# PSUM tiles for the first two chunks of a fused attention and channel-mix kernel: one tile of four banks, or one tile for each use with the four-bank tile laid over them later

## The chip, the cores and the metric

One core of a Trainium2 chip runs the kernel. The metric is device time in microseconds (us) for one execution; the median of the runs is given. Engines are called PE or TensorE (matrix products; PEld is its weight load), DVE or VectorE, ACT or ScalarE, POOL or GpSimd, and SP, which issues the DMAs. SBUF is the on-chip memory, and PSUM, of eight banks, is the memory that TensorE writes its products to. L12 is line 12 of the kernel.

## What is computed

Eight batches of 576 tokens go through attention with 8 heads of 64 against 72 keys and values, each the mean of 8 neighbours, and the result goes through a channel mix of width 512 with 1024 hidden units:

```
attn = softmax(q @ mean8(k).T / 8) @ mean8(v)          # q, k, v: [8, 8, 576, 64]
x    = attn, heads side by side                         # [8, 576, 512]
xk   = mu_k * x + (1 - mu_k) * x_prev                   # x_prev: x of the token before
xr   = mu_r * x + (1 - mu_r) * x_prev
out  = sigmoid(xr @ w_r) * (relu(xk @ w_k) ** 2 @ w_v)  # w_k: 512 x 1024, w_v: 1024 x 512, w_r: 512 x 512
```

## The kernel before

The 4608 tokens are worked in chunks of 128, 256 and then eleven of 384, and each chunk in tiles of 128 tokens: tile 0 is chunk 0, tiles 1 and 2 are chunk 1, tiles 3 to 5 chunk 2. For a tile, `softmax` and `part` make the scores on TensorE (`scores`, L791 and L799), then maxima (L839), subtraction (L856), exponential, sums and normalised weights. For a chunk, the attention product follows, and each product is turned by `shifted` (two ScalarE copies, scaled, L1080) and `joined` (two VectorE operations that read the same product again, L1122) into the two inputs xk and xr of the channel mix; `hidden` (L1177), `gate` (L1226) and `mixed` (L1259) are its matrix products.

The first two chunks take another way through PSUM than the rest. Their weights are transposed on TensorE (`transposed`, L933, and `transposed_rest`, L979) and copied to SBUF by ScalarE (L940, L986), and `attended` makes the attention product one pair of heads at a time (four pairs, L1066). Each of these uses one PSUM bank for a short while; they are called the small products here. From chunk 2 on VectorE transposes, and `quarters` (L1028) makes the product of all four pairs at once over four banks.

No instruction waits by hand. The order in which each engine gets its instructions is written out by a planner (`Order`, L131 to L241) while the kernel is built. Every piece of work is a generator. It says what it needs (`need`), takes a buffer from a list of free ones (`take`, with a kind such as "bank" or "sc") and names the engine and the length of the next step. Each generator has a due time, corrected by the table `EARLIER`. In each round the planner goes through the generators in the order of their due times and lets each take what is free; then, of the steps that are ready, it issues the one with the lowest due time on the engine that can start first. Of several free buffers of a kind it gives the one that has been free longest. The semaphores are added afterwards, from the tiles that the instructions read and write.

Four of the eight banks are one tile, `quad` (L378). Its banks 0 and 1 are handed out as the kind "sc", for the scores of a tile. Its banks 2 and 3 are handed out as two slots of the kind "bank", for the small products, and a tile of its own, `single`, is the third. `filling` takes `single` for the 40 filler products of L449, which run between the others until 47.43 us; so until then the small products alternate between banks 2 and 3. Three more banks, "mm", serve the channel mix. When the first two chunks are through, `four_banks` (L714) takes the three "bank" slots and gives banks 2 and 3 on as the kind "hi". `quarters` takes "sc" and "hi" together, and so do the scores of several tiles at once (through the view `wide`, L712). `single` becomes a fourth "mm" slot later.

What is due around this place: `gathered` of tile 3, which gives "sc" back, at 34 plus 232.6; `four_banks` at 18 plus 265.3; the scores of tile 4 at 39.4 plus 504.7.

Of the kernel before, what the change touches and what calls it, by code (L numbers as in the profile page):

```python
# [8 lines left out]
F32 = mybir.dt.float32  # L9
# [5 lines left out]
PSUM = bass.MemoryType.PSUM  # L15

P = 128
B, H, S, D = 8, 8, 576, 64
POOL = 8
KEYS = S // POOL  # L20
# [45 lines left out]
APART = 296  # L66
# [194 lines left out]
def attention_then_channel_mix(  # L261
# [15 lines left out]
    order = Order()  # L277
    need = lambda *what: ("need", *what)
    take = lambda kind: ("take", kind)
# [3 lines left out]
    banks = ctx.enter_context(tc.tile_pool(name="banks", bufs=1, space=PSUM))  # L283

    def slots(kind, n, shape, dtype=F32, pool=None):
        tiles = [(pool or const).tile(shape, dtype, name=f"{kind}{i}") for i in range(n)]
        for t in tiles:
            order.give(kind, t)
        return tiles
# [27 lines left out]
    def operand(kind, c):  # L317
        if c in WHOLE:
            return whole_operands[kind]
        if (kind, c) not in operands:  # L320
            whole = {"pth": range(len(CHUNKS)), "xkh": WHOLE_HID, "xrh": WHOLE_GATE, "sh": WHOLE_MIX, "ptq": range(len(CHUNKS))}.get(kind, ())
            dtype = F32 if c in whole else F32R
            operands[kind, c] = sb.tile(shapes[kind], dtype, name=f"{kind}_{c}", tag=kind)
        return operands[kind, c]
# [40 lines left out]
    for tag, n in EARLY:  # L365
        t = sb.tile([P, n, 2 * POOL * KEYS], F32, name=f"early_{tag}", tag=tag)
        for i in range(n):
            got = t[:, i]
# [6 lines left out]
        else:  # L375
            order.give(kind, slot)

    quad = banks.tile([P, 4, 512], F32, name="quad")  # L378
    order.give("sc", quad[:, :2])
    single, = slots("bank", 1, [P, 512], pool=banks)  # L380
    for a in (2, 3):
        order.give("bank", quad[:, a])
    slots("mm", 3, [P, 512], pool=banks)


    def stretches(at, n):
# [322 lines left out]
        done_with(kind, raw)  # L709
        order.make(("late rest", b))  # L710

    wide = quad.rearrange("p (a b) n -> p a (b n)", a=2)  # L712

    def four_banks():  # L714
        yield need(
            *[(k, i) for i, t in enumerate(tiles) if t[0] in WHOLE_ATT for k in ("main", "side")],
            *[("x", c, g, m) for c in WHOLE_ATT for g in range(NPAIR) for m in range(2)], "filled",
        )
        got = []
        for _ in range(3):  # L720
            got.append((yield take("bank")))
        order.give("hi", quad[:, 2:])
        yield need(("gating", FOURTH_FROM, 0))
        order.give("mm", single)

    def group_of(i):
        if i >= THREES_FROM:
            return [j for j, t in enumerate(tiles) if t[0] == tiles[i][0]]
        return list(TOGETHER) if i in TOGETHER else [i]

    def follows(i):
        return group_of(i)[0] != i

    def softmax(i):

        parts = tiles[i][2]
        if follows(i):
            yield need(("scores", i, 0))
            yield from part(i, 0, 2)
            return  # L740
        group = group_of(i)
        several = len(group) > 1
        if i:
            yield need(("scoring", i - 1))
            c = tiles[i if i >= THREES_FROM else max(group[-1] - 2, 0)][0] - 1
            if c >= 0 and c not in WHOLE_ATT:
                yield need(("attended", c, 0))
        yield need(*[("q", j) for j in group])
        yield need(
            *[("keys", b, p) for j in group for b, *_ in tiles[j][2] for p in range(1 if i in HALVED else 2)]  # L750
        )
        if several:
            held["four", tiles[i][0]] = [(yield take("sc")), (yield take("hi")), len(group)]
            for n, j in enumerate(group):
                view = wide[:, :, n * APART:n * APART + 4 * KEYS]
                held["halves", j] = view, None, [view[:, a:a + 1] for a in range(2)]
                order.make(("scoring", j))
            yield from part(i, 0, 2)
            return
        pair = None  # L760
        if i in BESIDE:
            pair = [(yield take("mm")), (yield take("mm"))]
            sc = None
            halves = [t.rearrange("p (a n) -> p a n", a=1) for t in pair]
        else:
            sc = yield take("sc")
            halves = [sc[:, a:a + 1] for a in range(2)]
        held["halves", i] = sc, pair, halves
        if i in HALVED:
            for kind in ("mx", "e", "sm", "px", "pm"):  # L770
                held[kind, i] = yield take(kind)
        order.make(("scoring", i))
        if i in HALVED:
            yield from part(i, 0, 1)
        else:
            yield from part(i, 0, 2)
# [224 lines left out]
    def ready(c):  # L1001
        mine = [i for i, t in enumerate(tiles) if t[0] == c]
        return (
            *[(k, i) for i in mine for k in ("main", "side")], "om",
            *([("rest", 0)] if c in WHOLE_ATT else [("late rest", b) for b, *_ in units[c]]),
            *[("values", b, p) for b, *_ in units[c] for p in range(2)], *([] if c in WHOLE_ATT else [("turned", b) for b, *_ in units[c]]),
        )

    def quarters(c):

        yield need(*ready(c))
        sc = yield take("sc")
        hi = yield take("hi")
        yield "pe", 2.75, False
        main = operand("pth", c).rearrange("p g n -> p (g n)").rearrange("p (i j k) -> p i j k", j=16, k=32)
        rest = operand("ptq", c)
        out = quad[:, :, :CH].rearrange("p t (g i k) -> p t g i k", g=NPAIR, k=32)
        batch = [next(b for b, _, n, at in units[c] if at <= CH // 4 * t < at + n) % 2 for t in range(4)]
        for g in range(NPAIR):
            for j in range(3):  # L1020
                for t, i in enumerate(batch):
                    rows = slice(32 * t, 32 * t + 32)
                    for m in range(2):
                        if j < 2:
                            w, p = vq_main[i][rows, (t - 2 * m - j) % 4, g], main[rows, :, 4 * g + 2 * m + j, :]
                        else:
                            w, p = vq_rest[i][rows, g // 2, 2 * (g % 2) + m], rest[rows, :, g // 2, :]
                        nc.tensor.matmul(  # L1028
                            out=out[m * D:(m + 1) * D, t, g], lhsT=w, rhs=p, start=(j == 0), stop=(j == 2),
                        )  # L1030
        for g in range(NPAIR):
            held["out", c, g] = quad[:, :, g * CH // 4:(g + 1) * CH // 4]
            order.make(("attended", c, g))
        held["quad", c] = [sc, hi, NPAIR]
# [265 lines left out]
    for i in range(NT):  # L1300
        spare = SPARE_THREE if i >= THREES_FROM else SPARE if tiles[i][0] > 1 else 0.0
        order.add(tile_due[i], softmax(i), spare)
        order.add(tile_due[i], gathered(i))
        if i in HALVED:
            order.add(tile_due[i] + 0.05, part(i, 1, 2), spare)
        order.add(tile_due[i] + 0.1, transposed(i), spare)
        order.add(tile_due[i] + 0.1, transposed_rest(i), spare)
    order.add(ATT[1] + 8, four_banks())
    for c, n in enumerate(CHUNKS):
        if c not in WHOLE_ATT:  # L1310
            order.add(att_due[c], quarters(c), SPARE)
        for g in range(NPAIR):
            order.add(att_due[c] + g, attended(c, g), SPARE if c > 1 else 0.0)
            if c in WHOLE:
                order.add(att_due[c] + g + 6, later_joined(c, g))
        for jt in range(NJT):
            order.add(begin[c] + 0.0455 * n * jt / NJT, hidden(c, jt), 1.0 if c else 0.0)
        for tt in range(n // P):
            order.add(begin[c] + 0.0455 * n + 2.8 * tt, gate(c, tt))
            order.add(begin[c] + (0.0455 + 0.022) * n + 5.5 * tt, mixed(c, tt))  # L1320
# [56 lines left out]
```

## Time and profile before

| | |
|---|---|
| median of 3 runs | 604.08 us (602.74 to 604.32) |
| profiled execution | 603.56 us, of which the span from the first to the last instruction is 601.7 us |
| TensorE busy | 590.3 us (98% of the span), 5822 products |
| VectorE, ScalarE, GpSimd busy | 347.7 (58%), 294.4 (49%), 223.4 (37%) |
| granted TensorE clock, mean | 0.999 |
| DMA | 54.72 MB, mean 91 GB/s |

Busy time is the time in which an engine executes an instruction. The 98% of TensorE are an average over the span: the page's 40 slices of some 15 us show it at 90% or more in all but the third (80 to 90%) and the last (70 to 80%, the tail, in which the last result is multiplied and written out). So the stretch from 30 to 45 us is the one to look into, by the views of the section below.

### The profile page before, as it was taken

Reading aid. Unit: us, or ns where it says so; the run is one execution under the profiler, and the core shown is the slowest. Engines: PE = TensorE matmul, PEld = TensorE weight load, DVE = VectorE, ACT = ScalarE, POOL = GpSimd, SP = SyncE. Lnnn points to the kernel's source line nnn. Section 1 sums busy time; section 2 is a strip of 40 time slices with the busy share of each in tenths; the row PEclk is TensorE's granted clock in tenths of the full one; section 3 lists DMA queues with packets and bytes.
Section 4 is the critical chain, followed back from the end, with each engine's and each line's share of the span. In section 5 each row is a group of like instructions: output and inputs, shape, how many; then the busy total and the mean of one; then the engine's idle time right before and its main releaser. Section 6 shows DMA issues by size and latency. Waiting matters only on the chain.

```text
span 601.7 us, 14119 instructions
## 1 busy us (share of the span) xinstructions
PE 590.3 (98%) x5822; PEld 508.9 (85%) x5822; DVE 347.7 (58%) x709; ACT 294.4 (49%) x574; POOL 223.4 (37%) x350
## 2 busy tenths in 40 slices
PE   9989999999999999999999999999999999999997
PEld 8868457888888988988988988988988988988985
DVE  4779975875626915854824853763833834833411
ACT  3656855755553452652652653553543553554420
POOL 2411058738234354247124248138215115115000
PEclk9999999999999999999999999999999999999999
DMA  8598242351006213321202421521200200000001
GB/s 302 200 345 338 84 143 74 113 187 59 23 1 213 69 38 106 114 71 57 76 2 72 150 71 51 198 71 48 86 2 36 71 2 36 19 2 36 19 0 52
DMA packets 23055, 54.72 MB, mean 91 GB/s; under 512 B 2896, under 2 KB 6352, under 8 KB 22992
## 3 DMA queue, kind: packets, MB, share of 16 engines
q1 hardware_dynamic: 22992, 53.82, 25.5%
q8 instruction: 46, 0.75, 0.5%
q14 instruction: 17, 0.14, 0.1%
HBM read 41.23 MB, written 9.44 MB: 84 GB/s over the span
## 4 chain that ended last, share of the span: by engine, by line
PE 84%; DVE 6%; POOL 4%; ACT 3%; issue 1%; DMA 1%; DVEq 0%; POOLq 0%; ACTq 0%
PE mm L1259 25%; PE mm L1177 24%; PE mm L1226 11%; PE bank L1177 6%; PE bank L1226 4%; PE quad L1028 4%; PE bank L1259 4%; PE quad L791 3%; POOL stage L575 1%; PE bank L449 1%; POOL xrl L1148 1%; PE mm L586 1%; POOL xkl L1148 1%; DVE sl L1202 1%; PE quad L1066 1%
## 5 line engine op out<-in xcount | busy, mean ns | idle before, releaser
L1177 PE MATMUL mm<-xkh,w_k 128*128 128x384 f32 x576 | 147.5, 336 | 1.2 <-DVE rk L1194 1.0
L1259 PE MATMUL mm<-w_v,sh 128*128 128x512 f32 x464 | 146.9, 392 | 0.0
L1122 DVE SCALAR_TENSOR_TENSOR xm<-quad,given,t 128x384 f32<-128x384 f32 x88 | 50.4, 613 | 112.3 <-ACT t L1080 75.7
L1177 PEld LDWEIGHTS mm<-xkh,w_k 128*128 128x128 f32 x576 | 103.5, 188 | 3.2 <-DVE rk L1194 1.7
L1259 PEld LDWEIGHTS mm<-w_v,sh 128*128 128x128 f32 x464 | 87.1, 188 | 19.1
L1177 PE MATMUL mm<-xkl,w_k 128*128 128x384 f32 x288 | 96.5, 335 | 0.5 <-POOL xkl L1148 0.5
L1259 PE MATMUL mm<-w_v,sl 128*128 128x512 f32 x232 | 90.4, 390 | 0.0
L1200 ACT CAST sh<-rk 128x384 fp32r<-128x384 f32 x88 | 45.1, 512 | 55.9 <-DVE rk L1194 55.7
L877 POOL TENSOR_TENSOR px<-e,sm 128x64 f32<-128x64 f32 (+1 forms) x33 | 13.7, 414 | 155.8 <-DVE sm L867 79.9
L1226 PE MATMUL mm<-w_r,xrh 128*128 128x512 f32 x192 | 61.3, 391 | 0.0
L1148 POOL TENSOR_TENSOR xkl<-xm,xkh 128x384 fp32r<-128x384 f32 x44 | 44.3, 1018 | 42.9 <-ACT xkh L1146 42.9
L1202 DVE TENSOR_TENSOR sl<-rk,sh 128x384 fp32r<-128x384 f32 x88 | 52.4, 596 | 12.8 <-ACT sh L1200 12.7
L1269 DVE TENSOR_TENSOR rs<-mm,rs 128x512 f32<-128x512 f32 x32 | 22.0, 688 | 64.6 <-PE mm L1259 64.2
L1080 ACT ACTIVATE t<-quad,om_sb 128x384 f32<-128x384 f32 (+1 forms) x96 | 48.2, 571 | 21.5 <-PE quad L1028 17.8
L1177 PEld LDWEIGHTS mm<-xkl,w_k 128*128 128x128 f32 x288 | 54.1, 188 | 1.1 <-POOL xkl L1148 1.1
L1187 ACT ACTIVATE rk<-mm 128x384 f32<-128x384 f32 x72 | 35.1, 487 | 39.2 <-PE mm L1177 38.1
L575 POOL TENSOR_TENSOR stage<-stage 128x512 f32<-128x512 f32 (+4 forms) x56 | 48.5, 869 | 7.1 <-DMA stage<-in_vm 4.9
L1259 PEld LDWEIGHTS mm<-w_v,sl 128*128 128x128 f32 x232 | 43.6, 188 | 8.7
L1148 POOL TENSOR_TENSOR xrl<-xm,xrh 128x384 fp32r<-128x384 f32 x44 | 44.3, 1017 | 3.0 <-ACT xrh L1146 3.0
L1194 DVE SCALAR_TENSOR_TENSOR rk<-mm,rk 128x384 f32<-128x384 f32 x72 | 39.7, 551 | 8.0 <-ACT rk L1187 6.8
L1226 PEld LDWEIGHTS mm<-w_r,xrh 128*128 128x128 f32 x192 | 36.0, 188 | 7.7
L1226 PE MATMUL mm<-w_r,xrl 128*128 128x512 f32 x96 | 37.5, 390 | 0.0
(154 smaller groups left out, 974.2 us busy)
## 6 DMA issues: line engine op xcount, KB each, us to landing
qs<-in_qT SPq DMA_DIRECT2D x36, 256.0 KB, 4.1
out<-rs SPq DMA_DIRECT2D x36, 256.0 KB, 2.0
stage<-in_kT SPq DMA_DIRECT2D x15, 576.0 KB, 5.5
stage<-in_vm SPq DMA_DIRECT2D x15, 512.0 KB, 5.5
got_wk<-in_w_k SPq DMA_DIRECT2D x8, 512.0 KB, 6.9
got_wv<-in_w_v SPq DMA_DIRECT2D x8, 512.0 KB, 9.8
stage<-in_vr SPq DMA_DIRECT2D x6, 512.0 KB, 4.0
got_wr<-in_w_r SPq DMA_DIRECT2D x4, 512.0 KB, 7.1
```

Of the source, the lines that this page charges most:

```text
L575: nc_eng.tensor_tensor(out=st[:, :, :w], in0=st[:, :, :w], in1=st[:, :, w:2 * w], op=ALU.add)
L1028: nc.tensor.matmul(out=out[m * D:(m + 1) * D, t, g], lhsT=w, rhs=p, start=(j == 0), stop=(j == 2),)
L1080: nc.scalar.activation(out=by_token(ts[m][:, 1:n + 1]), in_=xp, func=AF.Copy, scale=om_sb[:, m, g:g + 1])
L1122: nc.vector.scalar_tensor_tensor(out=by_token(xm[:, :n]), in0=bank[:, :n] if c in WHOLE_ATT else bank, scalar=mu_sb[:, m, g:g + 1], in1=by ...
L1148: nc.gpsimd.tensor_tensor(out=lo, in0=xm[:, :n], in1=hi, op=ALU.subtract)
L1177: nc.tensor.matmul(out=hp, lhsT=w[:, o], rhs=x[:, ct, :n], start=(ct == 0 and k == 0), stop=(ct == NCT - 1 and k == len(terms) - 1),)
L1187: nc.scalar.activation(out=rk[:, :n], in_=hp, func=AF.Relu)
L1194: nc.vector.scalar_tensor_tensor(out=rk[:, :n], in0=hp, scalar=0.0, in1=rk[:, :n], op0=ALU.max, op1=ALU.mult)
L1200: nc.scalar.copy(out=sh[:, :n], in_=rk[:, :n])
L1202: nc.vector.tensor_tensor(out=operand("sl", c)[:, jt, :n], in0=rk[:, :n], in1=sh[:, :n], op=ALU.subtract)
L1226: nc.tensor.matmul(out=bank, lhsT=x[:, ct, o], rhs=w, start=(ct == 0 and k == 0), stop=(ct == NCT - 1 and k == len(terms) - 1),)
L1259: nc.tensor.matmul(out=bank, lhsT=s[:, o], rhs=w, start=(jt == 0 and k == 0), stop=(jt == NJT - 1 and k == len(terms) - 1),)
```

## The change

Banks 0 and 1 become a tile for the scores ("sc"), and banks 2 and 3 become two tiles of one bank each ("bank"), all in a pool of their own. `four_banks` takes the three "bank" slots as before, then also "sc". It then closes that pool, opens another in its place with the tile of four banks, and gives its halves out as "sc" and "hi". `quarters` and the scores of several tiles reach the tile through a dictionary, since it does not exist yet when they are defined. The pool `banks` now holds `single` and the three "mm" tiles only. Nothing is computed otherwise.

```diff
-    quad = banks.tile([P, 4, 512], F32, name="quad")
-    order.give("sc", quad[:, :2])
     single, = slots("bank", 1, [P, 512], pool=banks)
+    slots("mm", 3, [P, 512], pool=banks)
+    beginning = ExitStack()
+    own = beginning.enter_context(tc.tile_pool(name="own", bufs=1, space=PSUM))
+    slots("sc", 1, [P, 2, 512], pool=own)
     for a in (2, 3):
-        order.give("bank", quad[:, a])
-    slots("mm", 3, [P, 512], pool=banks)
+        order.give("bank", own.tile([P, 512], F32, name=f"own{a}"))
+    joint = {}
...
-    wide = quad.rearrange("p (a b) n -> p a (b n)", a=2)
-
     def four_banks():
...
-        got = []
         for _ in range(3):
-            got.append((yield take("bank")))
+            yield take("bank")
+        yield take("sc")
+        beginning.close()
+        quad = ctx.enter_context(tc.tile_pool(name="joint", bufs=1, space=PSUM)).tile([P, 4, 512], F32, name="quad")
+        joint["quad"], joint["wide"] = quad, quad.rearrange("p (a b) n -> p a (b n)", a=2)
+        order.give("sc", quad[:, :2])
         order.give("hi", quad[:, 2:])
...
-                view = wide[:, :, n * APART:n * APART + 4 * KEYS]
+                view = joint["wide"][:, :, n * APART:n * APART + 4 * KEYS]
...
         rest = operand("ptq", c)
+        quad = joint["quad"]
         out = quad[:, :, :CH].rearrange("p t (g i k) -> p t g i k", g=NPAIR, k=32)
```

## Rows read from the trace of the kernel before

**Rows 1.** Busy time of each engine in two stretches (start:end, length, busy, instructions, clock).

```profile
20.00:44.20 24.20, 20.24 (x169) 17.18 (x167) 17.36 (x42) 14.70 (x43) 7.64 (x20) 1.00 0.79 275
44.20:80.00 35.80, 35.80 (x220) 23.06 (x221) 35.34 (x81) 24.35 (x45) 6.38 (x6) 1.00 0.58 214
```

**Rows 2.** Waits of TensorE from 60 us on (total us, times, longest us).

```profile
PE mm L1177 <- DVE rk L1194: 1.0, 1, 1.0
```

**Rows 3.** The chain that ended last, two stretches (start us, us, engine, tile, line).

```profile
40.14 0.50 DVE xkh L1122
...
42.06 0.85 ACT t L1080 x2
...
75.95 0.69 DVE rs L1269
...
152.51 10.18 PE mm L1177 x57
```

**Rows 4.** TensorE's instructions in order of time (start us, us; last, idle before and releaser).

```profile
25.61 0.66 PE L933 MATMUL quad<-ident,pm 128*128 128x128 f32 x4 [0.33 <-DVE stage L1122]
...
27.33 0.49 PE L1066 MATMUL quad<-whole_pth,vbd 128*128 128x128 f32 x2 [0.17 <-DVE stage L1122]
...
28.99 0.42 PE L979 MATMUL quad<-ident,pr 128*96 128x128 f32 x2 [0.32 <-ACT stage L1080]
...
33.51 0.70 PE L1066 MATMUL quad<-pth,vbd 128*128 128x256 f32 x2 [0.35 <-DVE stage L1122]
...
36.36 0.70 PE L1066 MATMUL quad<-pth,vbd 128*128 128x256 f32 x2 [0.47 <-DVE xrh L1122]
...
39.22 0.70 PE L1066 MATMUL quad<-pth,vbd 128*128 128x256 f32 x2 [0.69 <-DVE xrh L1122]
...
40.68 0.73 PE L791 MATMUL quad<-kbd,qs 64*64 64x72 f32 x32 [0.65 <-DVE xkh L1122]
...
44.13 1.13 PE L1177 MATMUL mm<-xkh,got_wk 128*128 128x256 f32 x4 [0.80 <-DVE xkh L1122]
...
87.93 7.03 PE L1259 MATMUL mm<-got_wv,stage 128*128 128x512 f32 x16
```

**Rows 5.** VectorE's instructions in order of time.

```profile
25.20 0.35 DVE L1122 SCALAR_TENSOR_TENSOR stage<-quad,given,stage 128x128 f32<-128x128 f32 x1 [0.69 <-ACT stage L1080]
...
27.92 0.35 DVE L1122 SCALAR_TENSOR_TENSOR stage<-quad,given,stage 128x128 f32<-128x128 f32 x1 [0.65 <-PE quad L1066]
...
33.10 0.35 DVE L1122 SCALAR_TENSOR_TENSOR stage<-quad,given,stage 128x128 f32<-128x128 f32 x1 [1.12 <-ACT t L1080]
...
34.43 0.48 DVE L1122 SCALAR_TENSOR_TENSOR xkh<-quad,given,t 128x256 f32<-128x256 f32 x1 [0.38 <-PE quad L1066]
...
35.82 0.48 DVE L1122 SCALAR_TENSOR_TENSOR xrh<-quad,given,t 128x256 f32<-128x256 f32 x1 [0.24 <-ACT t L1080]
...
38.33 0.43 DVE L540 TENSOR_SCALAR tmp<-tmp 128x512 int32<-128x512 int32 x1
...
42.93 0.76 DVE L839 TENSOR_REDUCE mx<-quad 128x8 f32<-128x576 f32 x1 [0.63 <-ACT t L1080]
...
46.59 0.75 DVE L856 TENSOR_TENSOR e<-quad,mx 128x576 f32<-128x576 f32 x1
...
79.40 0.72 DVE L856 TENSOR_TENSOR e<-quad,mx 128x576 f32<-128x576 f32 x1
```

**Rows 6.** ScalarE's instructions in order of time.

```profile
26.30 0.59 ACT L940 COPY pth<-quad 128x512 f32<-128x512 f32 x1 [1.13 <-PE quad L933]
...
34.95 0.84 ACT L1080 ACTIVATE t<-quad,om_sb 128x256 f32<-128x256 f32 x2 [1.13 <-DVE xkh L1122]
...
36.20 0.66 ACT L538 ACTIVATE tmp<-got_wk 128x512 f32<-128x512 f32 x1
...
60.65 0.69 ACT L538 ACTIVATE tmp<-got_wv 128x512 f32<-128x512 f32 x1
```

**Rows 7.** DMA issued between 45.6 and 47 us (KB each, us to landing).

```profile
got_wv<-in_w_v SPq DMA_DIRECT2D x1, 512.0 KB, 11.0
```

## The prediction

> **What bounds the kernel now.** I read the views in the order of the groups. The page has TensorE busy for 98% of the span, so the only time to be had is what it stands. The stretches say where: 24.20 − 20.24 = 3.96 us between 20 and 44.2 us, nothing between 44.2 and 80 [rows 1]. Later its longest wait is 1.0 us [rows 2]; the rest is start and tail. The granted clock is 1.00 in both stretches (the 2.4 GHz level), so neither gain nor loss comes from the clock.
>
> The chain of waits shows what the first stretch is made of [rows 3]: a ring of three engines. The scores of tile 3 (L791) read queries and the block of keys and write banks 0 and 1 of `quad`; they start at 40.68 and stood 0.65 us for the join L1122 of 40.14 [rows 3, 4], which reads a product in bank 2 or 3. The join after that waits until those scores end, and ScalarE's copy of the last product (42.06) until that join ends. None of the three needs the other's data or bank. They share only the tile `quad`: each access to it stands behind the last access of another engine to any of its banks, reads behind reads too. TensorE's list of stalls agrees: in several of its eight the named releaser works on another bank [rows 4].
>
> **The stalls, one by one.** They sum to 0.33 + 0.17 + 0.32 + 0.35 + 0.47 + 0.69 + 0.65 + 0.80 = 3.78 us [rows 4]. The fillers hold `single` until about 47 us, so the small products take turns on two banks; that stays. What changes is that each bank is a tile of its own, and a write waits for its own bank's readers. For each stall I ask whether the true releaser then comes early enough.
> - 25.61: transposes go into pair 0's bank, behind that pair's second join at 25.20. True, but the join had itself stood 0.69 us for ScalarE's copies of pair 1, in the other bank [rows 5]. 0.69 covers 0.33. Gain so far 0.33.
> - 27.33: pair 2 goes into the bank of those transposes, whose copy (26.30, 0.59 us) ends at 26.89 [rows 6]; the join that is named reads the other bank. TensorE was ready at 27.16, after 26.89, and both move up together. Gain 0.50.
> - 28.99: transposes into pair 1's bank. Its last join, 27.92 and 0.35 us long [rows 5], is over before TensorE was ready at 28.67; the copies named are pair 2's. Gain 0.82.
> - 33.51: pair 1 of chunk 1 stands behind the join of 33.10, which had stood 1.12 us for copies in the other bank [rows 5]. It would end at 33.45 − 1.12 = 32.33; TensorE is ready at 33.16 − 0.82 = 32.34. Gain 1.17.
> - 36.36: behind the join of 35.82. From the start of the join at 33.10 to the end of this one VectorE takes 3.20 us, 0.38 + 0.24 of it idle for the ring [rows 5]; 2.58 from 31.98 on is 34.56, and TensorE is ready at 35.89 − 1.17 = 34.72. ScalarE's copies at 34.95, which had stood 1.13 us for a join of the other bank [rows 6], no longer lie between. Gain 1.64.
> - 39.22: 0.89 us after the start of the shift at 38.33 [rows 5], whose join releases it. The shift needs ScalarE's conversion of 36.20 (0.66 us) [rows 6], which follows a ReLU of a TensorE product and so moves with TensorE, by 1.17: it ends at 35.69. 35.7 + 0.89 = 36.6, and TensorE is ready at 38.53 − 1.64 = 36.89. Gain 2.33.
> - 40.68: the scores need no bank that is in use. Gain 2.98.
> - 44.13: 1.20 us after the start of tile 3's maxima at 42.93 [rows 4, 5], with pair 3's join between. The maxima need the scores, which end at 40.68 + 0.73 − 2.98 = 38.43. Pair 3's product was done by 40.14 [rows 3], so now by 37.8, its copies (0.85) by 38.7. Even from 38.7 on it is 38.7 + 1.20 = 39.9; TensorE is ready at 43.33 − 2.98 = 40.35. Gain 3.78.
>
> All eight go. The margins are thinnest at 33.51 and 36.36 (0.0 and 0.2) and at 27.33 (0.3), but I have not counted there that VectorE, idle for 24.20 − 17.36 = 6.84 us of this stretch [rows 1], arrives earlier itself. The other 3.96 − 3.78 = 0.18 us are gaps without a named wait; they stay.
>
> Whether the program or the chip asks for a wait across banks, the rows cannot say. The Trainium skill (PSUM — Partial Sum Buffer, "PSUM bank collisions raise a hardware error") says that two engines must be kept apart on one bank, reads included, that different banks run clean, and that the chip neither arbitrates nor stalls. By that rule the waits across banks are the program's own, and rival 3 has no ground; no run here shows a collision.
>
> **What the change adds.** No compute instruction and no DMA. `four_banks` asks for one more slot, "sc", before the new tile is laid over the banks. Tile 3 holds that slot until its subtraction at 46.59, 0.75 us long [rows 5]. The thread that gives it back is due at 34 + 232.6 = 266.6, `four_banks` at 18 + 265.3 = 283.3, the scores of tile 4 at 39.4 + 504.7 = 544.1: served in that order, the slot goes on with an unchanged time, and I expect the order of the instructions to stay. The first write into the new tile is tile 4's scores, some 7 us after that subtraction; it waits for the last readers of all four banks, which have ended by then. Cost 0. Below zero it cannot go, since it lets nothing start sooner. If that cover went while the order held, the writer would stand for the rest of one reader, at most 0.75 us, with TensorE's hidden products queued behind it.
>
> **Does the gain last to the end?** From 44.2 to 80 us TensorE does not idle at all and VectorE for 35.80 − 35.34 = 0.46 us [rows 1], so VectorE could take back any gain that it does not share. It does share it: its maxima start by 38.7 instead of 42.93, 4.2 us earlier, against TensorE's 3.78. The weights are the other anchor. The last one was issued near 45.7 and landed 11.0 us later [rows 7], at 56.7; I take its conversion to be the fourth, at 60.65 [rows 6]. That leaves 3.95 us against 3.78, and the loads themselves come earlier, since the value load at the head of SP's queue waits for a halving of keys on VectorE. The chain from 75.95 to 152.51 has no TensorE in it [rows 3], but it begins where a TensorE product ends, so it moves as a whole; the 1.0 us wait at its end stays, give or take its own size.
>
> **The sum.** The profiled execution took 603.56 us. 603.56 − 3.78 = 599.8. The median of the runs shown, 604.08, lies 0.5 us above that execution, which would make it 600.3; between the two: 600.0.
>
> **Rivals.**
> 1. The thin margins do not hold. If 27.33, 33.51, 36.36 and 44.13 keep their waits, 0.17 + 0.35 + 0.47 + 0.80 = 1.79 us stay and 1.99 go: 602.0. For it: hardly any margin at two places. Against: VectorE's 6.84 idle us. 12%.
> 2. The gain is handed back. If VectorE comes to 44 us no earlier than now, it can close only its own 0.46 us before 80 us; TensorE stands for it, and the time is 603.1 to 603.6. For it: VectorE's full stretch and a chain of 76 us without TensorE. Against: VectorE's idle time before 44 us has the same cause. 6%.
> 3. The change does not do what it says: the waits across banks are not the shared tile's doing, and separate tiles keep them. 603.6 to 604.1. Against: the named releasers on other banks. 3%.
> 4. Slower: `four_banks` gets "sc" only after later tiles have had it. It decides once the slot comes free after the third of these, whose subtraction starts at 79.40 [rows 5]. Then the quarter products of chunk 2 are placed behind the block of 16 products at 87.93, 7.03 us long [rows 4]; chunk 2's inputs come as much later, TensorE stands for up to 7.03 us, and 599.8 + 7.0 = 606.8. Against it: the due times. 3%.
>
> **How the numbers follow.** The forecast has 76%, from 598.6 (the 0.18 us of gaps and the 1.0 us wait gained as well) to 601.2 (that wait doubled and 0.4 us more). Rival 1 reaches 602.0, with the runs' spread 602.4. The range 598.4 to 602.4 leaves out rivals 2 to 4 and the outer edge of the others. About 0.3% (1.8 us) is what a measurement can tell from no change, so faster begins below 602.3: the forecast and most of rival 1, 0.86; the same: rivals 2, 3 and the remainder, 0.10; slower 0.04.
>
> **What would show it.** In the new trace TensorE should have no stall between 20 and 41 us against an engine that works on another bank; tile 3's scores should follow the product before them at once, near 37.7; the hidden product of 44.13 should stand near 40.35; and all after it should lie some 3.8 us earlier, the restart of 152.51 near 148.7. If the early stalls go and 152.51 stays, rival 2 is right; if the stalls stay with the same releasers, rival 3; if the quarter products stand behind other products than now, rival 4.

## The result, and the profile after

The changed kernel took 598.05 us (median of 4 runs, 597.56 to 599.19), the kernel before 603.75 us beside it: a ratio of 0.991, 95% interval 0.9889 to 0.9931. Eleven later runs of the same changed kernel (e1, e9 below) ran from 597.43 to 600.44; over all fifteen the median is 598.38. So the direction and the place were as predicted, and the size was not: about 5.3 to 5.7 us in place of 4.1, and the first median lies 0.35 us below the range.

The profiled execution after took 597.71 us, its span is 595.8 us, 5.9 less than before. TensorE is busy for 588.2 us with the same 5822 products, against 590.3: a third of the gain is in *busy* time, which the prediction's sum, of idle time alone, left out.

Stretches of the kernel after (start:end, length, then busy time and instructions of TensorE, its weight loads, VectorE, ScalarE, GpSimd; granted clock; DMA share). The second answers to the first of [rows 1]:

```profile
14.00:20.00 6.00, 5.98 (x53) 5.79 (x52) 5.75 (x20) 5.25 (x16) 2.13 (x5) 1.00 0.74 264
20.00:40.40 20.40, 20.09 (x170) 18.28 (x169) 18.18 (x46) 14.99 (x43) 9.76 (x21) 1.00 0.81 295
40.40:76.00 35.60, 35.54 (x282) 21.80 (x282) 35.06 (x79) 24.78 (x43) 5.98 (x6) 1.00 0.65 243
```

About as many products, 170 for 169, fit into 20.40 us where they took 24.20 (not quite the same ones, since everything lies earlier by now), with 0.31 us of idle time where there were 3.96. The clock is the 2.4 GHz level (1.00) throughout, as before.

TensorE's instructions after, in order of time, at the places of [rows 4]:

```profile
23.38 0.60 PE L937 MATMUL own<-ident,pm 128*128 128x128 f32 x4
...
24.70 0.43 PE L1071 MATMUL own<-whole_pth,vbd 128*128 128x128 f32 x2
...
29.80 0.60 PE L1071 MATMUL own<-pth,vbd 128*128 128x256 f32 x2
...
32.47 0.70 PE L1071 MATMUL own<-pth,vbd 128*128 128x256 f32 x2 [0.30 <-DVE xrh L1127]
...
34.60 0.70 PE L1071 MATMUL own<-pth,vbd 128*128 128x256 f32 x2
...
35.35 0.73 PE L795 MATMUL sc<-kbd,qs 64*64 64x72 f32 x32
36.01 4.58 PE L1182 MATMUL mm<-xkh,got_wk 128*128 128x256 f32 x20
```

In this list seven of the eight bracketed stalls are gone; the one of 36.36 is left at 32.47. The hidden product that stood at 44.13 no longer begins a group of its own: it is within the twenty from 36.01 on. TensorE's waits of 0.3 us and more over the whole run (us, times, longest):

```profile
PE own L441 <- DVE tmp L437: 1.4, 1, 1.4
PE mm L1182 <- DVE rk L1199: 0.9, 1, 0.9
PE mm L1182 <- POOL xkl L1153: 0.5, 1, 0.5
PE own L1071 <- DVE xrh L1127: 0.3, 1, 0.3
```

The first three were there before, within 0.1 us of this size ([rows 2] has the second).

**Where 5.93 us come from when 3.78 were shown.** Line the two traces up product by product. From the first key sums on TensorE (7.29 us before, 6.82 after) to the last filler products (46.83 and 40.43) it is 39.54 and 33.61 us: 5.93 less. The view that shows these 5.93 us is that of the weight loads (PEld), which the prediction did not read. Before:

```profile
16.97 0.42 PEld L933 LDWEIGHTS quad<-ident,pm 128*128 128x128 f32 x4 [0.29 <-POOL pm L882]
19.71 0.17 PEld L979 LDWEIGHTS quad<-ident,pr 128*96 128x96 f32 x2 [0.26 <-issue]
23.48 0.30 PEld L1066 LDWEIGHTS quad<-whole_pth,vbd 128*128 128x128 f32 x2 [0.33 <-ACT pth L940]
24.56 0.30 PEld L1177 LDWEIGHTS mm<-stage,got_wk 128*128 128x128 f32 x2 [0.23 <-DVE stage L1122]
25.61 0.42 PEld L933 LDWEIGHTS quad<-ident,pm 128*128 128x128 f32 x4 [0.52 <-DVE stage L1122]
27.33 0.30 PEld L1066 LDWEIGHTS quad<-whole_pth,vbd 128*128 128x128 f32 x2 [0.36 <-DVE stage L1122]
28.98 0.17 PEld L979 LDWEIGHTS quad<-ident,pr 128*96 128x96 f32 x2 [0.46 <-ACT stage L1080]
33.51 0.30 PEld L1066 LDWEIGHTS quad<-pth,vbd 128*128 128x128 f32 x2 [0.54 <-DVE stage L1122]
36.36 0.30 PEld L1066 LDWEIGHTS quad<-pth,vbd 128*128 128x128 f32 x2 [0.67 <-DVE xrh L1122]
37.82 0.30 PEld L1177 LDWEIGHTS mm<-xkh,got_wk 128*128 128x128 f32 x2 [0.17 <-DVE xkh L1122]
39.21 0.30 PEld L1066 LDWEIGHTS quad<-pth,vbd 128*128 128x128 f32 x2 [1.09 <-DVE xrh L1122]
40.68 0.58 PEld L791 LDWEIGHTS quad<-kbd,qs 64*64 64x64 f32 x32 [0.95 <-DVE xkh L1122]
44.13 2.02 PEld L1177 LDWEIGHTS mm<-xkh,got_wk 128*128 128x128 f32 x10 [1.20 <-DVE xkh L1122]
```

and after, in the same stretch:

```profile
32.46 0.30 PEld L1071 LDWEIGHTS own<-pth,vbd 128*128 128x128 f32 x2 [0.50 <-DVE xrh L1127]
34.60 0.30 PEld L1071 LDWEIGHTS own<-pth,vbd 128*128 128x128 f32 x2 [0.41 <-DVE xrh L1127]
35.34 0.58 PEld L795 LDWEIGHTS sc<-kbd,qs 64*64 64x64 f32 x32 [0.23 <-issue]
```

The brackets of before add up to 7.07 us, those of after to 1.14; the difference is 5.93. That it agrees to the last digit is chance, but the same sum comes close in the other profiles: against the kernel before it gives 5.75 us in e1 below for 5.73 measured, 2.12 in e3 for 2.04, 5.16 in e4 for 5.28, 5.81 in e7 for 5.81, and 0.31 us more time in e2 for 0.32. Two things are to be seen. Five places show a stall here at which the list of the products shows none (16.97 to 24.56, and 37.82). At every other place the bracket is 0.14 to 0.40 us longer than in [rows 4]: 0.52 against 0.33 at 25.61, 1.20 against 0.80 at 44.13. Without a stall the next weight load starts about 0.1 us ahead of its product, and that product about 0.16 us before the modelled end of the one before; with a stall, load and product start together after the releaser. By this view three stalls are left after, not one: the load at 34.60, the place of 39.22, still stands 0.41 us for VectorE, and that of the scores 0.23.

**What was handed back.** From tile 4's scores to the first gate product it is 6.00 us before (53.44 to 59.44) and 6.44 after (47.04 to 53.48). From the first key sums to the end of the span 594.4 − 589.0 = 5.4 us of the 5.93 are left. The other 0.47 us of the profiled 5.9 lie at the start, before any small product: the first fourteen filler passes (a filler product shows as two passes) took 2.42 us before and 1.95 after.

### The profile page after: what moved, and what is told of

It reads as the page before. It is cut to its first block, busy times and chain, and to the rows that moved or that the text cites. A ratio compares the mean times of both kernels' runs of the same rounds, so it can differ in the third digit from the quotient of the medians.

```text
span 595.8 us, 14121 instructions
## 1 busy us (share of the span) xinstructions
PE 588.2 (99%) x5822; PEld 508.3 (85%) x5822; DVE 348.5 (58%) x709; ACT 294.3 (49%) x574; POOL 224.9 (38%) x350
## 4 chain that ended last, share of the span: by engine, by line
PE 84%; DVE 5%; POOL 4%; DMA 3%; ACT 2%; issue 1%; SPq 1%; DVEq 0%; POOLq 0%; ACTq 0%
PE mm L1264 26%; PE mm L1182 24%; PE mm L1231 11%; PE bank L1182 6%; PE quad L1033 4%; PE bank L1231 4%; PE bank L1264 4%; PE quad L795 3%; DMA got_wr<-in_w_r 2%; POOL stage L577 1%; POOL xkl L1153 1%; POOL xrl L1153 1%; PE own L441 1%; DVE xm L1127 1%; DVE stage L577 1%
## 5 line engine op out<-in xcount | busy, mean ns | idle before, releaser
L1207 DVE TENSOR_TENSOR sl<-rk,sh 128x384 fp32r<-128x384 f32 x88 | 53.4, 608 | 12.8 <-ACT sh L1205 12.7
L1085 ACT ACTIVATE t<-quad,om_sb 128x384 f32<-128x384 f32 x88 | 44.9, 580 | 17.7 <-PE quad L1033 17.7
L1199 DVE SCALAR_TENSOR_TENSOR rk<-mm,rk 128x384 f32<-128x384 f32 x72 | 39.6, 550 | 8.3 <-ACT rk L1192 7.2
```

Of the source, the lines that this page charges most:

```text
L1085: nc.scalar.activation(out=by_token(ts[m][:, 1:n + 1]), in_=xp, func=AF.Copy, scale=om_sb[:, m, g:g + 1])
L1199: nc.vector.scalar_tensor_tensor(out=rk[:, :n], in0=hp, scalar=0.0, in1=rk[:, :n], op0=ALU.max, op1=ALU.mult)
L1207: nc.vector.tensor_tensor(out=operand("sl", c)[:, jt, :n], in0=rk[:, :n], in1=sh[:, :n], op=ALU.subtract)
```

## The experiments

Spans within the profiles are measured from the first key sums, to leave that start out: A is the time from there to the last filler products, B the time from tile 4's scores to the first gate product, E the time from the first key sums to the span's end.

| kernel | filler passes at 5 us | A | B | E | median of runs (lowest to highest) | ratio to before, 95% interval |
|---|---|---|---|---|---|---|
| before | 2.42 | 39.54 | 6.00 | 594.4 | 603.75 | |
| after | 1.95 | 33.61 | 6.44 | 589.0 | 598.05 (597.56 to 599.19) | 0.9889 to 0.9931 |
| e1 after again | 2.31 | 33.81 | 6.14 | 588.9 | 598.67 (597.45 to 600.44) | 0.9900 to 0.9930 |
| e2 one tile | 2.37 | 39.86 | 6.00 | 594.9 | 603.83 (602.86 to 604.39) | 0.9987 to 1.0004 |
| e3 scores apart | 1.86 | 37.50 | 6.00 | 592.7 | 601.48 (600.94 to 601.57) | 0.9944 to 0.9970 |
| e4 scores with one | 2.72 | 34.26 | 6.32 | 590.2 | 598.59 (597.45 to 599.68) | 0.9896 to 0.9921 |
| e7 four late | 2.22 | 33.73 | 6.02 | 588.9 | 597.74 (596.77 to 601.72) | 0.9886 to 0.9936 |
| e8 weights sooner | 2.27 | 33.68 | 6.04 | 588.6 | 598.41 (597.12 to 599.72) | 0.9898 to 0.9925 |
| e9 after again | 2.15 | 33.95 | 6.59 | 590.7 | 598.26 (597.43 to 599.62) | 0.9898 to 0.9925 |
| e10 join first | 2.32 | 33.35 | 6.69 | 589.1 | 598.42 (597.53 to 599.84) | 0.9907 to 0.9932 |
| e11 both | 1.72 | 34.15 | 6.59 | 590.4 | 597.55 (597.51 to 598.56) | 0.9892 to 0.9919 |
| e12 split later | 2.02 | 33.92 | 6.24 | 590.2 | 598.68 (597.57 to 602.04) | 0.9905 to 0.9952 |
| e13 split sooner | 1.75 | 34.44 | 6.31 | 590.7 | 598.81 (597.82 to 601.24) | 0.9905 to 0.9946 |
| e14 all three | 2.48 | 33.46 | 6.43 | 590.1 | 599.57 (597.93 to 600.27) | 0.9912 to 0.9943 |

### e1: the changed kernel again

> The changed kernel as it is, a second profile and more times. Theory (the waits across the banks of one tile, and each costs more than the idle time shown before it): 597.6 to 598.6 us; TensorE busy near 588.2 us and its idle time near 7.6 us as in the first profile. The first 0.47 us (the 14 filler products at 5.03 take 1.95 us here and 2.42 us in the kernel before, with no wait shown) are not of the change: over several profiles of both kernels the filler stretch should take either value in either kernel. Rival (placement of the pools decides): the filler stretch takes 1.95 us in every kernel with the new pools.

A and E repeat (33.81, 588.9), and the filler passes do not: 2.31 us here with the new pools, and over the fifteen profiles with the new pools anything from 1.72 to 2.72, with the 2.42 us of the old pools well within. The 0.47 us at the start are not the change's; the rival falls.

### e2: one tile in the new pools

```diff
-    slots("sc", 1, [P, 2, 512], pool=own)
+    four = own.tile([P, 4, 512], F32, name="four")
+    order.give("sc", four[:, :2])
     for a in (2, 3):
-        order.give("bank", own.tile([P, 512], F32, name=f"own{a}"))
+        order.give("bank", four[:, a])
```

> The new pools, the new closing and the late tile stay, but the scores' two banks and the two small banks are one tile of four banks again until the late tile is laid over. Theory (shared tile): all eight waits come back, 603.0 to 604.3 us, TensorE busy near 590.3 us and idle near 11.4 us. Rival (placement of the pools or banks, or when the four banks are handed over, gave part of the gain): 597.6 to 602, by as much as that part is.

603.83 us against 603.70 for the kernel before beside it, TensorE busy for 590.4. All eight stalls are back, at 0.34, 0.48, 0.33, 0.35, 0.47, 0.69, 0.65 and 0.80 us, with the releasers of [rows 4]; the last two are

```profile
40.94 0.73 PE L796 MATMUL four<-kbd,qs 64*64 64x72 f32 x32 [0.65 <-DVE xkh L1128]
...
44.40 2.86 PE L1183 MATMUL mm<-xkh,got_wk 128*128 128x256 f32 x12 [0.80 <-DVE xkh L1128]
```

The pools, their place and the late tile are worth nothing by themselves that these runs can tell (0.8 us at most, by the interval); the sharing of one tile is the cause.

### e3 and e4: parts of the split

```diff
 # e3
-        order.give("bank", own.tile([P, 512], F32, name=f"own{a}"))
+    two = own.tile([P, 2, 512], F32, name="two")     # banks two[:, 0] and two[:, 1]
 # e4
+    three = own.tile([P, 3, 512], F32, name="three") # sc is three[:, :2], one bank three[:, 2]
+    order.give("bank", own.tile([P, 512], F32, name="own3"))
```

> Only the scores get a tile of their own; the two small banks share one tile. Theory: the six stalls up to 39.22 of the kernel before stay, as far as they are between the two small banks (their true size, by the shift of TensorE's starts: 2.87 us, and 1.2 us from 16 to 25 us); the two at 40.68 and 44.13 (0.71 and 1.07 us by the shift) go: about 602.0 us, 600.8 if the shifts of 16 to 25 us came from the scores' readers. Rival (each stall is worth only the idle time shown, 0.65 + 0.80): 602.3 us. Rival (the ring needs all four banks, any split breaks it): 598 us.

> The scores share a tile with one of the two small banks, and the other small bank has a tile of its own. Theory: the waits between the two small banks go (2.87 us by the shift of TensorE's starts), those of the scores with the shared bank stay as far as it is that bank whose reader comes late, half of 1.78 us as a guess: 599 to 600.5 us. Rival (ring needs all four banks): 598 us. Rival (the scores' readers, long as they are, are the costly ones): 602 us.

In e3 six of the eight stalls stay at their old sizes, and the scores follow the pair before them at once:

```profile
38.12 0.70 PE L1072 MATMUL two<-pth,vbd 128*128 128x256 f32 x2 [0.70 <-DVE xrh L1128]
38.47 0.47 PE L1072 MATMUL two<-ptr,vbd_r 96*128 96x256 f32 x1
38.87 0.73 PE L796 MATMUL sc<-kbd,qs 64*64 64x72 f32 x32
```

A falls by 2.04 us: 0.54 before the first pair of chunk 1 and the rest, 1.5, at the two places of 40.68 and 44.13, where [rows 4] shows 0.65 + 0.80. In e4 five of those six go. Left are that of 36.36, as in the changed kernel, and a part of the hidden product's:

```profile
33.33 0.70 PE L1072 MATMUL own<-pth,vbd 128*128 128x256 f32 x2 [0.40 <-DVE xrh L1128]
...
39.15 2.86 PE L1183 MATMUL mm<-xkh,got_wk 128*128 128x256 f32 x12 [0.28 <-DVE xkh L1128]
```

A falls by 5.28, more than expected. So the ring between the two small banks is the larger part, and the scores' tile alone gives 2.2 us (603.70 − 601.48). That any split breaks everything falls with e3. For e4 the profile shows a rest of the ring, but its median (598.59) cannot be told from the changed kernel's beside it (598.67).

### e5 and e6: what one stall costs

A tail behind all other products: 24 groups of four filler products, each followed by a small VectorE copy out of the bank just written.

```diff
+        for i in range(24):
+            for _ in range(4):
+                nc.tensor.matmul(out=halves[i % 2][:, :P], lhsT=ident, rhs=ident, start=True, stop=True)
+            nc.vector.tensor_copy(out=small[:, 0, :, 0], in_=halves[i % 2][:, :4])
 # e5: halves are two tiles of one bank;  e6: halves are the two halves of one tile
```

> The changed kernel with a tail added after all its own products: 24 groups of four filler products of 128x128, in turn into two banks, each group followed by a VectorE copy of four columns of the bank just written. Here the two banks are two tiles. Theory: no stall, since a group waits only for the copy of the group before the last; the 24 groups follow one another at the fillers' pace, about 0.24 us a product or 0.95 us a group, 23 us in all. It is the base for the next run.

> The same tail, but the two banks are the two halves of one tile (the two last banks of the four-bank tile). Theory: every group now waits for the copy of the group before it, which reads the other bank, so TensorE stalls 23 times, some 0.2 to 0.4 us of shown idle time each. The theory on the price says that a group comes later by the idle time shown and another 0.16 us (the overlap with the group before, lost) and up to 0.1 us (its first product longer): if the shown idle is 0.3, the tail is 23 x 0.5 = 11 to 13 us longer than with two tiles. Rival (a stall costs what is shown before it): 23 x 0.3 = 7 us longer. Rival (no wait across the banks of one tile): as long as with two tiles.

Two neighbouring groups in e5, two in e6, and a weight load of e6:

```profile
592.39 1.06 PE L1292 MATMUL mm<-ident 128*128 128x128 f32 x8
593.28 1.06 PE L1292 MATMUL bank<-ident 128*128 128x128 f32 x8
```

```profile
594.18 1.16 PE L1292 MATMUL quad<-ident 128*128 128x128 f32 x8 [0.25 <-DVE mx L1294]
595.59 1.16 PE L1292 MATMUL quad<-ident 128*128 128x128 f32 x8 [0.25 <-DVE mx L1294]
```

```profile
612.54 0.97 PEld L1292 LDWEIGHTS quad<-ident 128*128 128x128 f32 x8 [0.44 <-DVE mx L1294]
```

With two tiles a group comes every 0.893 us (from 592.39 to 612.04, 22 steps); with one tile, every 1.413 us (592.76 to 623.84). That is 0.52 us a stall where the bracket shows 0.25: 0.25 shown, 0.17 of overlap lost (1.06 − 0.893) and 0.10 by which the group is longer (1.16 against 1.06). 23 × 0.52 = 12.0 us, and the spans differ by 626.4 − 614.5 = 11.9 (one profiled execution of each). Both rivals (7 us, 0 us) fall. The weight load's bracket, 0.44, comes closer than the product's.

### e7: the four-bank tile later still

```diff
-            *[("x", c, g, m) for c in WHOLE_ATT for g in range(NPAIR) for m in range(2)], "filled",
+            *[("x", c, g, m) for c in WHOLE_ATT for g in range(NPAIR) for m in range(2)], "filled", ("scoring", 6),
...
-    order.add(ATT[1] + 8, four_banks())
+    order.add(tile_due[6] + EARLIER.get("gathered 6", 0.0) - EARLIER.get("four_banks", 0.0) + 0.01, four_banks())
```

> The step that lays the four-bank tile over the own tiles waits until tile 6 has its scores' slot, and its due time puts it right behind tile 6 in the planner, one tile later than in the changed kernel as it came out (where it is served after tile 5). The order of instructions on every engine is the same. Theory (when the tile is handed over does not matter as long as the order is kept): 597.6 to 598.8 us, as the changed kernel. Rival (my fourth: a late hand-over puts chunk 2's quarter products behind a block of 16 products): 605 us.

In the changed kernel the first write into the new tile is that of tile 6's scores; tiles 4 and 5 still use the own one:

```profile
60.54 0.73 PE L795 MATMUL sc<-kbd,qs 64*64 64x72 f32 x32
...
64.83 0.73 PE L795 MATMUL quad<-kbd,qs 64*64 64x72 f32 x32
```

In e7 tile 6 uses the own one too, and A, B, E and the median (597.74) lie among those of the changed kernel. The later hand-over costs nothing that shows here.

### e8, e10, e11: the rest of the gain

e8 and e11 issue gate weights sooner; e10 and e11 put the join that 32.47 waits for ahead of a halving of keys.

```diff
 # e8, e11: order of the loads
-k3 wk5 wk6 wk7 wr0 q4 q5 wr1 v3 wr2 wr3
+k3 wk5 wk6 wk7 wr0 wr1 q4 wr2 q5 v3 wr3
 # e10, e11: the planner's steps, written out, one of them moved
...
-keys 1 1, hidden 0 4, loads, hidden 0 4, hidden 0 3, attended 1 0,
+hidden 0 4, loads, hidden 0 4, hidden 0 3, attended 1 0, keys 1 1,
...
```

> In the changed kernel two of the gate's weights are issued earlier by SP: the second before two loads of queries, the third before the last of these and the values, by 1 to 3 us; nothing else moves in any engine's order. Theory (about 0.4 us of the gain are handed back between 47 and 53.5 us, because ScalarE's conversions of these weights at 37.30, 40.23 and 44.07 stand 0.69, 0.58 and 0.45 us for the DMAs): these waits shrink or go, TensorE's first gate product comes 5.7 us after the product of tile 4's scores at most, and the time is 597.3 to 598.2 us, up to 0.4 us less than the changed kernel's. Rival (VectorE's full queue there sets the pace, not the DMAs): the conversions start sooner and nothing else moves. Rival (queries late instead): the scores of tile 4 at 47.04 come later.

> In the changed kernel one pair of VectorE instructions is exchanged: the join that the product of 32.47 waits for goes ahead of the halving of keys that stands 0.82 us for its DMA. All other orders are the same. Theory (a stall costs what it shows, 0.3 to 0.5 us, and another 0.25): TensorE has no stall from 20 to 41 us, and the filler products of 40.43 come 33.1 us or less after the start of the sums of 6.82 (33.61 and 33.81 us in the first two profiles). Second theory (the weights' landing holds the first gate product at about 53.45 us): that product does not come earlier, so the time stays at 597.5 to 599 us. Rival (no anchor there): the time falls with the front, by 0.5 us.

> The exchange of the run before and the two gate weights issued sooner by SP, together. If the weights' landing holds the first gate product at about 53.45 us, it comes earlier here, to some 6.0 us after the product of tile 4's scores (the kernel before took 6.00 from 53.44 to 59.44), and the time is 0.4 to 0.5 us less than the changed kernel's: 597.0 to 598.3 us. Rival (VectorE's full queue holds it): it stays at 53.4 to 53.5 us as in the run before, and the time as well.

e10 takes the stall of 32.47 away, and a smaller one comes up at the next pair; A falls by 0.26 to 0.46 us, and the first gate product stands for VectorE at 53.83:

```profile
34.70 0.70 PE L1434 MATMUL own<-pth,vbd 128*128 128x256 f32 x2 [0.32 <-DVE xrh L1490]
...
53.83 7.13 PE L1594 MATMUL mm<-got_wr,xrh 128*128 128x512 f32 x16 [0.32 <-DVE sh L1562]
```

So what the front gains is handed back there: something holds that product at 53.4 to 53.8 us (53.48 after, 53.44 in e7, 53.73 in e1). With the weights issued sooner (e8) ScalarE's conversions at 39.91 and 44.01 no longer wait for a DMA, and the gate product comes at 53.46 all the same: B is 6.04, not the 5.7 that I wrote down. That does not clear the weights, though. 5.7 was out of reach, since 6.00 us is what TensorE's own products take there without a stall (before, e2, e3, e5). And e8 moved the second and third gate weights and left the first where it was, which in the changed kernel reads

```profile
37.30 0.67 ACT L540 ACTIVATE tmp<-got_wr 128x512 f32<-128x512 f32 x1 [0.69 <-DMA got_wr<-in_w_r]
...
38.00 0.43 DVE L542 TENSOR_SCALAR tmp<-tmp 128x512 int32<-128x512 int32 x1 [0.60 <-ACT tmp L540]
```

ScalarE stands for that weight and VectorE for ScalarE, where neither stood before (42.78 and 43.99): SP issued the load only 0.72 us sooner, at 28.73 in place of 29.45. From there on VectorE is full (busy for 35.06 of the 35.60 us from 40.4 on), and shortly before the gate product, at 51.48, a weight load stands 0.46 us for it. Roughly, B goes with VectorE's wait at that place: 6.00 us where there is none (before, e3, e5), 6.02 to 6.32 at 0.30 to 0.47 (e1, e4, e6, e7, e8, e12), 6.43 to 6.69 at 0.60 to 0.81 (after, e10, e14). So the late weight and VectorE's full queue, which I had set against each other, seem to act together. This is read off the profiles; the first gate weight was not moved by itself. The profile of e11 cannot tell, since another stall lay in it (next).

### e9, e12 to e14: why the runs spread

> The changed kernel as it is, beside the next two on the same chip: 597.5 to 599 us; the stall that is left before the product of 32.47 (0.30 us in the first profile, 0.49 in the second) is there again, since VectorE's halving of keys ahead of the join stands for a DMA.

The third profile of the very same kernel was 1.9 us longer than the first (span 597.7), with stalls that the first does not have:

```profile
25.93 1.25 ACT L540 ACTIVATE tmp<-got_wk 128x512 f32<-128x512 f32 x2 [1.14 <-DMA got_wk<-in_w_k]
...
28.50 0.42 PE L983 MATMUL own<-ident,pr 128*96 128x128 f32 x2 [0.97 <-ACT ptr L990]
...
42.81 5.45 PE L1182 MATMUL mm<-xkh,got_wk 128*128 128x256 f32 x24 [1.24 <-DVE sh L1199]
```

The first two belong together: a weight lands late, ScalarE converts it late, and its next copy, which frees a small bank, is late as well. e5 and e13 show the same (0.80 and 1.42 us at 28.4 and 28.6). Before, the corresponding conversion, at 26.79, waited for no DMA. The third has two causes in VectorE's queue. The first gate weight landed later still (VectorE stood 1.48 us at 39.33, against 0.60 in the first profile), and behind it there is a collision. L1199, which TensorE waits for, comes 2.41 us later than in the first profile (42.35 and 39.94), 1.33 by the later start and 1.07 by the collision. VectorE and GpSimd near it, in e9 and then in the first profile:

```profile
40.67 1.76 DVE L545 SCALAR_TENSOR_TENSOR got_wk<-got_wk,tmp 128x512 int32<-128x512 int32 x1
...
40.16 1.72 POOL L570 TENSOR_TENSOR w_k<-got_wk,w_k 128x512 fp32r<-128x512 f32 x1 [2.78 <-ACT w_k L567]
```

```profile
39.34 0.69 DVE L545 SCALAR_TENSOR_TENSOR got_wk<-got_wk,tmp 128x512 int32<-128x512 int32 x1
...
39.44 1.73 POOL L570 TENSOR_TENSOR w_k<-got_wk,w_k 128x512 fp32r<-128x512 f32 x1 [2.52 <-ACT w_k L567]
```

In e9 GpSimd was under way first and VectorE's instruction took 1.76 us; in the first profile VectorE was first by 0.1 us and took 0.69. The Trainium skill (SBUF — State Buffer, "Who interferes with whom") says that a VectorE instruction with two SBUF inputs contends with a GpSimd instruction that reads SBUF, that the port pair they share is an exclusive lock, and that the issue order decides who blocks. The trace agrees: VectorE's instruction takes 1.76 us as the later one and 0.69 as the first, and GpSimd's as the later one is the longer the closer it follows (1.82 us in e10, 0.01 us behind; 1.40 in e1, 0.43 us behind). e12 and e13 move GpSimd's instruction, by exchanging the rounding on ScalarE that releases it with a ReLU beside it; e14 adds e11's edits to e12.

```diff
 # the planner's steps, written out, one of them moved
-hidden 1 0, loads, hidden 1 2, split k 0, convert k 6, hidden 1 2, loads, hidden 1 1,
 # e12, e14
+hidden 1 0, loads, hidden 1 2, convert k 6, hidden 1 2, loads, hidden 1 1, split k 0,
 # e13
+split k 0, hidden 1 0, loads, hidden 1 2, convert k 6, hidden 1 2, loads, hidden 1 1,
```

> In the changed kernel one pair of ScalarE instructions is exchanged: the rounding of a weight (L567), behind which GpSimd's subtraction (L570) starts, goes behind the next ReLU, so that GpSimd starts some 0.7 us later, near 40.2 us, when VectorE's L545 is mostly done. All other orders are the same. Theory (the collision of the two makes the slower runs): L545 takes 0.7 us in the profile, TensorE does not stand for VectorE near 42 us, and the runs lie closer together, 597.0 to 598.5 us with a median near 597.6. Rival (the spread comes from the DMAs' landing alone): the spread stays, 597.4 to 600, median 598.3.

> The same instruction of ScalarE exchanged the other way, ahead of the ReLU before it: GpSimd's subtraction starts near 38.6 us, ahead of VectorE's L545 or L542. Theory (collision): in the profile one VectorE instruction near 38.7 to 39.5 us takes 1.7 us or so in place of 0.4 to 0.7, TensorE stands 0.5 to 1.3 us near 41 to 43 us, and the median is 598.8 to 599.8 us. Rival (no collision): 598.3 us as the changed kernel.

> The later rounding of e12 with the join ahead of the halving and the gate's weights issued sooner (e11). Theory: TensorE stands neither near 32 nor near 42 us, the first gate product comes 46.0 to 46.4 us after the sums (46.66 and 46.56 us in the first two profiles of the changed kernel), and the time is 596.8 to 598 us, at or below the changed kernel's fastest runs. Rival (what holds the first gate product is VectorE's full queue): 597.5 to 598 us, no better than e12.

The collision can be made and taken away. In e13, with GpSimd ahead, it is there; in e12 VectorE's L545 takes 0.69 us (at 39.50). The lines of e13, whose kernel has 363 lines more, so that L545 and L570 are L908 and L933:

```profile
38.58 1.53 DVE L908 SCALAR_TENSOR_TENSOR got_wr<-got_wr,tmp 128x512 int32<-128x512 int32 x1
...
38.30 1.27 POOL L933 TENSOR_TENSOR w_k<-got_wk,w_k 128x512 fp32r<-128x512 f32 x1 [0.83 <-ACT w_k L930]
```

But the spread does not follow it. e12 runs from 597.57 to 602.04 with a median of 598.68, e13's median is 598.81, and e13's profile shows no stall of TensorE near 42 us. In e14 the front is about as short as in e10 (A 33.46), and the gate product comes 46.50 us after the key sums, not the 46.0 to 46.4 expected; its median, 599.57, is the highest of all versions, and its profile has another wait of 1.02 us for VectorE at 139.07. The collision lengthens VectorE's instruction by 0.8 to 1.1 us in three profiles (e9, e11, e13), with a stall of TensorE behind it in two (1.24 us in e9, in part the late weight's, and 0.71 in e11); it does not explain the runs as a whole, and no version here beats the changed kernel: e11's lower median (597.55) has an interval that overlaps e1's.

## Why the prediction was right, and where it failed

- **The mechanism: right.** e2 brings every stall back by the sharing alone, and the chain's ring [rows 3] is gone. That TensorE now writes one bank while others are read, with nothing but the program's waits removed, is what rival 3 denied.
- **The sum: this step failed.** The terms 0.33 + … + 0.80 = 3.78 took the idle time before the products for the price of a stall. The price is that plus the overlap lost with the group before (0.16 to 0.17) plus up to 0.10 of a longer first product; e6 measures 0.52 for 0.25. The same eight places are worth 0.55, 0.40, 0.54, 0.51, 0.18, 0.73, 0.71 and 1.07 us in the shift of TensorE's starts, 4.69 together, although some of them keep a part of their stall.
- **"The other 0.18 us are gaps without a named wait; they stay": wrong.** Four stalls from 17.00 to 24.57, too short for a bracket, go with the sharing too and give 1.21 us (0.29, 0.30, 0.31, 0.31); in e2 the brackets of their loads are back, at 0.29, 0.26, 0.33 and 0.22. Not all of them are waits for a bank: the load at 24.56 waits for its input, which a join wrote late. With the 4.69 they make 5.90 of the 5.93 us.
- **"All eight go": not all.** 36.36 keeps 0.30 us (0.3 to 0.6 in most other profiles), and by its load 39.22 keeps 0.41. For 36.36 I moved VectorE's whole series of 2.58 us forward; a halving of keys within it waits for its DMA, which SP issued only 0.72 us sooner (26.92 in place of 27.64):

```profile
31.26 0.76 DVE L577 TENSOR_TENSOR stage<-stage 128x576 f32<-128x576 f32 x1 [0.82 <-DMA stage<-in_kT]
31.93 0.48 DVE L1127 SCALAR_TENSOR_TENSOR xrh<-own,given,t 128x256 f32<-128x256 f32 x1
```

- **The hand-over.** The order of the instructions stayed, as said. That the slot goes on right after tile 3 was wrong. It went after tile 5: `four_banks` waits for the fillers too, and their bank came free a moment after the slot. Rival 4 took that for a loss; e7 delays it once more at no cost, past tile 6, the third of the later tiles, so its point of decision was wrong too.
- **Does the gain last?** Mostly: 5.4 of 5.93 us. The margin that I found, 3.95 us against 3.78, does not cover 5.93, and 0.44 us come back at the first gate product (0.00 to 0.69 in the other profiles). Rival 2 is thus right for a small part of the gain. The weight that I took for the anchor, the last value weight, was not the one: the profiles point to the first gate weight, passed on by VectorE's full queue, which no run tried by itself. The wait of 1.0 us at the restart stayed (0.9; the restart is at 146.61, not near 148.7).
- **The range.** Its lower end allowed for the 0.18 and 1.0 us only. An unknown price per stall, times twelve stalls, was not among the bounds. That the time lies only just below the range is luck in part: the front gave 2.15 us more than the sum had (5.93 for 3.78), and 0.44 of it were handed back by a wait that the sum did not have either.

## What to carry to other kernels

Read a TensorE stall off its weight loads, not off its products: the idle time before the load is nearer to what the stall costs, and stalls that show no bracket on the product are seen there. Banks that different engines use at different times belong in tiles of their own, since a shared tile makes readers wait for readers. When a ring of waits goes, the work moves up by several us, and loads and shared ports that had slack before have to be counted again at the new size.

## What the runs showed of the hardware

One short stall among small products costs 0.52 us where 0.25 us of idle time is shown (e6 against e5). A VectorE and a GpSimd instruction that meet come out at 0.69 and 1.40 to 1.82 us where VectorE's is first (after, e1, e7, e10), and at 1.53 to 1.76 and 1.27 to 1.72 us where GpSimd's is (e9, e11, e13); GpSimd's took 1.31 us at 45.84 in the kernel before, where VectorE's was all but done by then. The first filler products after the start take 1.72 to 2.72 us for the same fourteen passes, at no visible wait. What makes runs of one kernel of this group differ by 1 to 5 us is not settled: late weights and the collision were each seen in profiles, and in e4, e12 and e13 a second wait for GpSimd near 91 us.
